# Linear attention feeding two MLPs on one core: scans read from PSUM, chunk 3 moved behind the first matmul step, VectorE priority for the first chunks, and filler matmuls in four gaps

## The chip, the core and the metric

The program runs on one NeuronCore of a Trainium2 chip. The metric is device time in microseconds (us). Six parts of the core matter here. [...] VectorE (DVE), ScalarE (ACT) and GpSimd (POOL) do elementwise work; GpSimd does not read PSUM. The queue of SyncE (SP) issues most of the DMA transfers, and each engine and queue works through its instructions in its own fixed order.

## The reference

The input has 4 batches, 8 heads, 768 positions and a head size of 48. First comes a gated linear attention, then two MLPs over the 3072 tokens (model width 384, hidden width 2048):

```python
for t in range(S):
    state = alpha[:, :, t, :, None] * state + einsum('bhd,bhe->bhde', k[:, :, t], v[:, :, t])
    y[:, :, t] = einsum('bhd,bhde->bhe', q[:, :, t], state)
x = y as (3072, 384)
h = x @ moe_w_in;   g = where(h >= 1, h, where(h <= -1, 0, (h + 1)**2 / 4));   x = g @ moe_w_out
h = x @ moe2_w_in;  g = maximum(0.01 * h, h);                                 out = g @ moe2_w_out
```

The MLP weights arrive as float64, so the kernel reads them as pairs of 32-bit words and builds float32 values itself.

## The kernel before

**Attention.** The 3072 tokens are cut into 24 chunks of 128 positions (chunk c is batch c mod 4). The recurrence becomes products of alpha inside a chunk. For a chunk, PE transposes alpha, k and q into PSUM (`transposed`, tiles `Tal`, `Tk`, `Tq`, L269). `st_alpha` copies `Tal` to the SBUF tile `al` on ACT (L278) and runs two long scans on DVE over all four head pairs at once: one backwards into `kt` (L284), one forwards into `qt` (L288), which starts from the reciprocal of the total product. The second operand of both scans is `init`, a tile of zeros whose column 0 restarts each head pair. `st_k` and `st_q` multiply `Tk` and `Tq` into `kt` and `qt`. `st_scores` multiplies `kt` and `qt` on PE (tiles `sc`) and masks them on DVE into `S` (L329). `st_ktok` transposes `kt` back, `st_kv` updates the state, and `st_y` makes the output `y` on PE (L365, L372), from which ACT and DVE build the two halves of `xt`, the input of the first MLP: first a part `xs` (L380) that six DMAs move into place (L387), then the rest (L382).

**Weights.** Each layer has 28 weight pieces in four groups: three pieces of w_in, then four of w_out in each. A piece is loaded (`raw`, four buffers), prepared by ACT (L29, L30), DVE (L31, L32) and POOL (L35), joined on DVE (L40), and split into a high and a low part by ACT and by POOL or DVE (L185, L189). One `tick` issues one stage of three neighbouring pieces.

**GEMM steps.** Three chunks make a tile of 384 tokens; a layer has eight tiles of 16 steps. Step m is nine matmuls into `h` (L445, `gemm_in`), the activation on ACT, DVE (`t`, L458), ACT and POOL into `gg`, and three steps later nine matmuls into `acc` (L485, `gemm_out`). `h` has two PSUM buffers, so the `h` of step m+2 waits until DVE has made `t` of step m. Steps 0 to 3 need the first weight group, steps 4 to 7 the second, and so on.

**What sets the order.** PE's order is written out by hand. The prelude is the string `PRE`: words such as `al.0` or `y.1` are attention stages of a chunk and `t` is a tick. Then the step loop issues gemm_out of step i-3, the planned attention stages, the hooks (ticks) and gemm_in of step i. `VISITS` puts the stages of a tile's next three chunks at half-step slots 0, 3 and 5, each chunk nine slots after the last. In the prelude `bank` hands out all eight PSUM banks in rotation; later attention has three. The order on DVE, ACT, POOL and SP is decided by a list scheduler at build time, by priority and its own estimate of times; only `st_y` raises a priority (`PRIO_Y`).

The second layer runs from about 550 us on and is not touched.

Of the kernel before, what the change touches and what calls it, by code (L numbers as in the profile page):

```python
# [7 lines left out]
F32 = mybir.dt.float32  # L8
# [4 lines left out]
ACTF = mybir.ActivationFunctionType  # L13
# [49 lines left out]
def fast_path(ctx, tc, q, k, v, alpha, w1i, w1o, w2i, w2o, out, wz, in_range):  # L63
# [55 lines left out]
    HD = H * D  # L119
    vs = [stp.tile([128, HD + X], F32, name=f"v{i}") for i in range(2)]  # L120
    nats = [stp.tile([128, 3, H, HP], F32, name=f"nat{i}") for i in range(2)]
    al = stp.tile([R, NP, C + 1], F32, name="al")
    init = stp.tile([R, NP, C + 1], F32, name="init")
    heads = [slice(HP * e, HP * e + D) for e in range(2)]

    fetched = set()
# [129 lines left out]
    def bank(nm):  # L256
# [5 lines left out]
            return ph.tile([128, 512], F32, tag="h", name=nm)  # L262
        return pa.tile([128, 512], F32, tag=f"acc{i - 5}", name=nm)

    def transposed(c, i):
        t = nats[c % 2][:, i]
        ps = bank(("Tal", "Tk", "Tq")[i])
        for a in range(NP):
            nc.tensor.transpose(  # L269
                ps[:R, a * C:(a + 1) * C],  # L270
                t[:, 2 * a:2 * a + 2, :].rearrange("p two d -> p (two d)")[:, :R],
                ident,
            )
        return ps[:R].rearrange("p (a t) -> p a t", a=NP)

    def st_alpha(c):
        ps = transposed(c, 0)
        nc.scalar.activation(out=al[:, :, 1:], in_=ps, func=ACTF.Copy)  # L278
        kt = tp.tile([R, NP, C + 1], F32, tag="kt", name="kt")
        qt = tp.tile([R, NP, C + 1], F32, tag="qt", name="qt")  # L280
        alf, inf, ktf, qtf = (t.rearrange("p a t -> p (a t)") for t in (al, init, kt, qt))
        n = NP * (C + 1)
        nc.gpsimd.memset(kt[:, NP - 1, C:], 1.0)
        nc.vector.tensor_tensor_scan(ktf[:, n - 2::-1], alf[:, n - 1:0:-1], inf[:, n - 1:0:-1], 1.0, ALU.mult, ALU.add)  # L284
        tot = tots[:, c]
        nc.vector.tensor_scalar(out=tot, in0=kt[:, :, :1], scalar1=TOT_MIN, scalar2=None, op0=ALU.max)  # L286
        nc.vector.reciprocal(out=init[:, :, :1], in_=tot)
        nc.vector.tensor_tensor_scan(qtf, alf, inf, 0.0, ALU.mult, ALU.add)  # L288
        nc.gpsimd.memset(init[:, :, :1], 1.0)
        if c >= B:  # L290
            st = states[c % B]
            for h in heads:
                nc.gpsimd.tensor_tensor(  # L293
                    out=st[h, :, h], in0=st[h, :, h], in1=tot[h].to_broadcast([D, NP, D]), op=ALU.mult
                )
        cs[c] = {"kt": kt[:, :, 1:], "qt": qt[:, :, 1:]}

    def st_k(c):
        ps = transposed(c, 1)
        kt = cs[c]["kt"]  # L300
        nc.vector.tensor_tensor(out=kt, in0=ps, in1=kt, op=ALU.mult)

    def st_q(c):
        ps = transposed(c, 2)
        load_qka(c + 2)
        qt = cs[c]["qt"]
        nc.vector.tensor_tensor(out=qt, in0=ps, in1=qt, op=ALU.mult)
# [13 lines left out]
    def st_scores(c):  # L321
        kt, qt = cs[c]["kt"], cs[c]["qt"]
        ps = [bank(f"sc{e}") for e in range(2)]
        for a in range(NP):
            for e, h in enumerate(heads):
                nc.tensor.matmul(ps[e][:, a * C:(a + 1) * C], kt[h, a, :], qt[h, a, :])  # L326
        S = sp.tile([128, 2, NP, C], F32, tag="S", name="S")
        for e in range(2):
            nc.vector.tensor_tensor(  # L329
                out=S[:, e],  # L330
                in0=ps[e].rearrange("p (a t) -> p a t", a=NP),
                in1=causal.rearrange("p (o t) -> p o t", o=1).to_broadcast([128, NP, C]),
                op=ALU.mult,
            )
# [77 lines left out]
    def stage(nm, c):  # L412
        if c < NCH:
            stages[nm](c)
# [147 lines left out]
    with tc.manual_schedule(engines={mybir.EngineType.PE}):  # L562
# [238 lines left out]
```

## Time and profile before

| | |
|---|---|
| median of three runs | 1004.99 us (1003.87 to 1006.16) |
| the profiled execution | 1004.65 us, of which the trace spans 1002.6 us |
| PE busy | 948.6 us, 95% of the span |
| DVE, ACT, POOL busy | 458.1, 476.6, 404.2 us |
| PE busy by fortieths of the span | `4567889999999999999999999999999999999997` |
| granted PE clock by fortieths | `9879889999999999999999999999999999999999` |

Each digit is a tenth of a slice of 25 us. PE is full from the seventh slice to the last; only the first six, some 130 us, have room. The share of a whole span says nothing about these six, so the rows below are by stretch.

### The profile page before, as it was taken

Reading aid. Unit: us, or ns where it says so; the run is one execution under the profiler, and the core shown is the slowest. Engines: PE = TensorE matmul, PEld = TensorE weight load, DVE = VectorE, ACT = ScalarE, POOL = GpSimd, SP = SyncE. Lnnn points to the kernel's source line nnn. Section 1 sums busy time; section 2 is a strip of 40 time slices with the busy share of each in tenths; the row PEclk is TensorE's granted clock in tenths of the full one; section 3 lists DMA queues with packets and bytes.
Section 4 is the critical chain, followed back from the end, with each engine's and each line's share of the span. In section 5 each row is a group of like instructions: output and inputs, shape, how many; then the busy total and the mean of one; then the engine's idle time right before and its main releaser. Section 6 shows DMA issues by size and latency. Waiting matters only on the chain.

```text
span 1002.6 us, 16502 instructions
## 1 busy us (share of the span) xinstructions
PE 948.6 (95%) x6226; PEld 928.2 (93%) x6226; DVE 458.1 (46%) x781; ACT 476.6 (48%) x950; POOL 404.2 (40%) x440
## 2 busy tenths in 40 slices
PE   4567889999999999999999999999999999999997
PEld 3466889999999999999999999999999999999997
DVE  6889854546555556465552455323331212121211
ACT  3566644464655555546555773333333333333332
POOL 4558853243444443435442333333333333333332
PEclk9879889999999999999999999999999999999999
DMA  9866623235443443354313435111110000000000
GB/s 171 175 160 141 151 49 64 46 97 111 110 120 84 99 124 74 106 113 118 89 39 110 130 105 172 40 56 41 56 40 32 24 1 24 1 25 1 25 1 27
DMA packets 134807, 79.02 MB, mean 79 GB/s; under 512 B 105536, under 2 KB 123456, under 8 KB 134720
## 3 DMA queue, kind: packets, MB, share of 16 engines
q1 hardware_dynamic: 122624, 52.71, 24.0%
q10 hardware_dynamic: 12096, 25.17, 8.4%
q8 instruction: 51, 0.84, 0.3%
q14 instruction: 36, 0.29, 0.1%
HBM read 59.77 MB, written 15.73 MB: 75 GB/s over the span
## 4 chain that ended last, share of the span: by engine, by line
PE 83%; DVE 7%; DMA 5%; ACT 2%; SPq 2%; issue 1%; DVEq 0%; ACTq 0%
PE h L445 37%; PE acc L487 19%; PE acc L485 18%; PE y L372 2%; PE sc L326 2%; DMA raw<-in_moe_w_in 2%; PE y L365 2%; DVE z L40 1%; DMA x2r<-x2d 1%; PE Tq L269 1%; DVE z L31 1%; DMA v<-in_v 1%; PE Tk L269 1%; PE Tal L269 1%; DVE kt L284 1%
## 5 line engine op out<-in xcount | busy, mean ns | idle before, releaser
L463 POOL TENSOR_TENSOR gg<-t,gg 128x384 fp32r<-128x384 f32 x256 | 274.7, 1074 | 458.5 <-ACT gg L462 453.5
L445 PE MATMUL h<-xt,wi 128*128 128x384 f32 x2304 | 448.5, 338 | 5.8 <-DVE t L458 3.0
L445 PEld LDWEIGHTS h<-xt,wi 128*128 128x128 f32 x2304 | 405.9, 190 | 9.2 <-DVE t L458 3.5
L485 PE MATMUL acc<-gg,wo 128*128 128x384 f32 x1152 | 227.4, 341 | 0.8 <-ACT o L498 0.8
L487 PE MATMUL acc<-wo,gg 128*128 128x384 f32 x1152 | 219.9, 334 | 0.0
L462 ACT ACTIVATE gg<-t 128x384 fp32r<-128x384 f32 x256 | 134.1, 524 | 177.3 <-DVE t L458 99.9
L485 PEld LDWEIGHTS acc<-gg,wo 128*128 128x128 f32 x1152 | 202.6, 190 | 3.4 <-ACT o L498 1.5
L487 PEld LDWEIGHTS acc<-wo,gg 128*128 128x128 f32 x1152 | 201.5, 188 | 0.0
L461 DVE TENSOR_TENSOR t<-h,t 128x384 f32<-128x384 f32 x128 | 71.1, 557 | 266.6 <-ACT t L460 266.4
L460 ACT ACTIVATE t<-h 128x384 f32<-128x384 f32 x128 | 62.9, 492 | 173.4 <-PE h L445 170.9
L458 DVE SCALAR_TENSOR_TENSOR t<-t,h 128x384 f32<-128x384 f32 x128 | 70.3, 549 | 138.4 <-ACT t L457 135.0
L456 ACT ACTIVATE t<-h,half 128x384 f32<-128x384 f32 x128 | 74.0, 578 | 94.9 <-PE h L445 93.1
L35 POOL TENSOR_TENSOR z<-z,raw 128x384 int32<-128x384 int32 (+1 forms) x56 | 67.9, 1213 | 48.6 <-DVE z L32 25.3
L457 ACT ACTIVATE t<-t 128x384 f32<-128x384 f32 x128 | 67.0, 523 | 4.0 <-ACT t L456 1.2
L284 DVE TENSOR_TENSOR_SCAN kt<-al,init 112x515 f32<-112x515 f32 x24 | 35.5, 1480 | 34.1 <-ACT al L278 34.1
L293 POOL TENSOR_TENSOR state<-state,good 48x192 f32<-48x192 f32 x40 | 26.2, 656 | 50.1 <-DVE good L286 42.9
L40 DVE SCALAR_TENSOR_TENSOR z<-raw,z 128x384 int32<-128x384 int32 (+1 forms) x56 | 41.2, 737 | 3.3 <-POOL z L35 3.3
L372 PE MATMUL y<-S,v 128*64 128x128 f32 (+1 forms) x384 | 30.4, 297 | 12.6 <-issue 5.3
L29 ACT ACTIVATE raw<-raw 128x384 int32<-128x384 uint32 (+1 forms) x56 | 33.7, 601 | 17.7 <-DMA raw<-in_moe_w_in 16.3
L31 DVE TENSOR_SCALAR z<-z 128x384 f32<-128x384 f32 (+1 forms) x56 | 27.7, 495 | 26.3 <-ACT z L30 26.2
L372 PEld LDWEIGHTS y<-S,v 128*64 128x64 f32 (+1 forms) x384 | 23.1, 139 | 17.2 <-issue 5.5
L288 DVE TENSOR_TENSOR_SCAN qt<-al,init 112x516 f32<-112x516 f32 x24 | 35.6, 1483 | 0.6
(70 smaller groups left out, 607.0 us busy)
## 6 DMA issues: line engine op xcount, KB each, us to landing
raw<-in_moe_w_out SPq DMA_DIRECT2D x16, 384.0 KB, 4.7
raw<-in_moe_w_in ACTq DMA_DIRECT2D x12, 512.0 KB, 4.3
raw<-in_moe_w_out ACTq DMA_DIRECT2D x16, 384.0 KB, 3.5
nat<-in_alpha SPq DMA_DIRECT2D x24, 192.0 KB, 3.4
nat<-in_k SPq DMA_DIRECT2D x24, 192.0 KB, 4.2
nat<-in_q SPq DMA_DIRECT2D x24, 192.0 KB, 4.4
raw<-in_moe_w_in SPq DMA_DIRECT2D x24, 192.0 KB, 4.0
v<-in_v SPq DMA_DIRECT2D x24, 192.0 KB, 3.2
```

What stands on the lines that cost most here:

```text
L35: add_eng.tensor_tensor(out=z, in0=z, in1=low, op=ALU.add)
L372: nc.tensor.matmul(y[HP * e:HP * e + n, a, :], vs[c % 2][:, (2 * a + e) * D:(2 * a + e) * D + n], d["S"][:, e, a, :], start=first and a == ...
L445: nc.tensor.matmul(h, w[:, wl, kk, f0:f0 + 128], xt[:, kk, xl, :], start=cnt == 0, stop=cnt == 3 * KD - 1,)
L456: nc.scalar.activation(out=t, in_=h, func=ACTF.Relu, bias=half, scale=0.5)
L457: nc.scalar.activation(out=t, in_=t, func=ACTF.Square)
L458: gi = nc.vector.scalar_tensor_tensor(out=g, in0=t, scalar=1.0, in1=h, op0=ALU.min, op1=ALU.max)
L460: nc.scalar.activation(out=t, in_=h, func=ACTF.Copy, scale=0.01)
L461: gi = nc.vector.tensor_tensor(out=g, in0=h, in1=t, op=ALU.max)
L462: hi = nc.scalar.activation(out=gg[:, HI], in_=g, func=ACTF.Copy)
L463: lo = nc.gpsimd.tensor_tensor(out=gg[:, LO], in0=g, in1=gg[:, HI].bitcast(F32), op=ALU.subtract)
L485: nc.tensor.matmul(acc[d][:, :N], w[:, wl, mi, d * 128:(d + 1) * 128], gg[:, xl], start=st, stop=sto)
L487: nc.tensor.matmul(acc[d][:, :DM], gg[:, xl, d * C:(d + 1) * C], w[:, wl, mi, :], start=st, stop=sto)
```

## The change

There are five edits.

1. The scans read `Tal` in PSUM. The ACT copy into `al` and the tiles `al` and `init` go. Each of the two scans becomes four scans of 128 columns, one for each head pair, with a column of zeros read with stride 0 as second operand and the start value given as an operand.
2. Chunk 3's `al k q` leave the prelude and are planned between the `h` of step 0 and step 1.
3. `BEHIND` moves the attention visits of the first three tiles back by 6, 4 and 2 half-steps.
4. In the prelude the scans, the products into `kt` and `qt` and the mask into `S` get the raised priority (`urgent`). After the prelude it has no offset.
5. Four words `w` in the prelude issue nine matmuls of the identity matrix each, into a PSUM bank that nobody reads.

```diff
+    zcol = const.tile([R, 1], F32, name="zcol")
+    zeros = zcol.to_broadcast([R, C])
...
-    al = stp.tile([R, NP, C + 1], F32, name="al")
-    init = stp.tile([R, NP, C + 1], F32, name="init")
...
+    def urgent():
+        return tc.high_priority(offset=PRIO_Y if prelude[0] else 0)
...
-        nc.scalar.activation(out=al[:, :, 1:], in_=ps, func=ACTF.Copy)
...
-        nc.vector.tensor_tensor_scan(ktf[:, n - 2::-1], alf[:, n - 1:0:-1], inf[:, n - 1:0:-1], 1.0, ALU.mult, ALU.add)
...
-        nc.vector.tensor_tensor_scan(qtf, alf, inf, 0.0, ALU.mult, ALU.add)
...
+        with urgent():
+            for a in range(NP):
+                nc.vector.tensor_tensor_scan(pad[:, a, C + 2:2:-1], ps[:, a, ::-1], zeros, 1.0, ALU.mult, ALU.add)
...
+            for a in range(NP):
+                nc.vector.tensor_tensor_scan(qt[:, a, :], ps[:, a, :], zeros, rtot[:, a, :], ALU.mult, ALU.add)
...
-        "al.0 k.0 q.0 t al.1 k.1 q.1 t kt.0 sc.0 t y.0 kv.0 al.2 k.2 q.2 t kt.1 sc.1 t y.1 kv.1 t "
-        "kt.2 sc.2 t al.3 k.3 q.3 t y.2 kv.2 t "
+        "al.0 k.0 q.0 t w al.1 k.1 q.1 t kt.0 sc.0 w t y.0 kv.0 al.2 k.2 q.2 t kt.1 sc.1 w t y.1 kv.1 t "
+        "kt.2 sc.2 t w t y.2 kv.2 t "
...
+    BEHIND = (6, 4, 2)
...
+            elif word == "w":
+                ps = bank("keep_warm")
+                for _ in range(9):
+                    nc.tensor.matmul(ps[:, :128], ident, ident)
...
-        plan = {}
+        plan = {(1, 0): [lambda w=w: stage(w, 3) for w in ("al", "k", "q")]}
...
-                    slot += i * SLOTS // n
+                    slot += i * SLOTS // n + (BEHIND[j] if j < len(BEHIND) else 0)
```

On PE before, the start of the step loop reads as follows; `wi_249` is the first group of w_in, `y<-S,v_125` belongs to chunk 3.

```order
L314 MATMUL ktok<-ident,kt 128x112 x4
L326 MATMUL sc_560<-qt,kt 128x128
L326 MATMUL sc_561<-qt,kt 128x128
...
L445 MATMUL h<-xt,wi_249 128x384 x18
L372 MATMUL y<-S,v_125 64x128
```

On PE after, the same place, right behind the last state product of chunk 2:

```order
L352 MATMUL kv<-v_125,kn 48x48
L453 MATMUL h<-xt,wi_266 128x384 x9
L272 MATMUL Tal<-ident,nat_128 112x128 x4
L272 MATMUL Tk<-ident,nat_128 112x128 x4
L272 MATMUL Tq<-ident,nat_128 112x128 x4
L453 MATMUL h<-xt,wi_266 128x384 x18
L493 MATMUL acc_738<-gg,wo_426 128x384
```

The scores of chunk 3 stood ahead of the first GEMM step; now its transposes stand behind it, and its scores behind the first `acc`.

On DVE before, these are the rows up to the last part of chunk 2's `xt`; `kt<-al` and `qt<-al` scans around them are chunk 3's, and `wi_550` and the 512-wide `z` are pieces of the second weight group.

```order
L286 TENSOR_SCALAR good<-kt 112x4
L301 TENSOR_TENSOR kt<-Tk,kt 112x4x128
L287 RECIPROCAL init<-good 112x4
L189 TENSOR_TENSOR wi_550<-z,wi_550 128x512
L288 SCALAR_TENSOR_TENSOR qt<-al,init 112x516
L31 TENSOR_SCALAR z<-z 128x512
L380 TENSOR_TENSOR xs<-y,xs 112x128
L307 TENSOR_TENSOR qt<-Tq,qt 112x4x128
L32 TENSOR_SCALAR z<-z 128x512
L382 TENSOR_TENSOR xt<-y,xt 112x3x128
```

On DVE after, the rows up to the same part of chunk 2's `xt`; `sc_482` and `sc_483` are chunk 2's scores, the first `xs` and `xt` are chunk 1's, and the 384-wide `z` are the four w_out pieces of the first group.

```order
L336 TENSOR_TENSOR S<-sc_482,causal 128x512
L387 TENSOR_TENSOR xs<-y,xs 112x128
L336 TENSOR_TENSOR S<-sc_483,causal 128x512
L40 SCALAR_TENSOR_TENSOR z<-raw,z 128x384
L389 TENSOR_TENSOR xt<-y,xt 112x3x128
L40 SCALAR_TENSOR_TENSOR z<-raw,z 128x384 x2
L189 TENSOR_TENSOR wo_426<-z,wo_426 128x384
L31 TENSOR_SCALAR z<-z 128x384
L32 TENSOR_SCALAR z<-z 128x384
L387 TENSOR_TENSOR xs<-y,xs 112x128
L40 SCALAR_TENSOR_TENSOR z<-raw,z 128x384
L389 TENSOR_TENSOR xt<-y,xt 112x3x128
```

Chunk 2's `xs` and `xt` moved ahead of chunk 3's scans and of all pieces of the second weight group.

On DVE before, at the end of the weight conversion (the last two `L40` rows; `state_121` and `xs` are chunk 5's, the first `t` is that of step 10, the `kt` scan is chunk 6's):

```order
L355 TENSOR_TENSOR state_121<-kv,state_121 48x4x48 x2
L31 TENSOR_SCALAR z<-z 128x384
L458 SCALAR_TENSOR_TENSOR t<-t,h 128x384
L380 TENSOR_TENSOR xs<-y,xs 112x128
L32 TENSOR_SCALAR z<-z 128x384
L189 TENSOR_TENSOR wo_1171<-z,wo_1171 128x384
L40 SCALAR_TENSOR_TENSOR z<-raw,z 128x384
L382 TENSOR_TENSOR xt<-y,xt 112x3x128
L40 SCALAR_TENSOR_TENSOR z<-raw,z 128x384
L284 SCALAR_TENSOR_TENSOR kt<-al,init 112x515
L458 SCALAR_TENSOR_TENSOR t<-t,h 128x384
```

On DVE after, the same end (here the `t` are those of steps 12 and 13; `state_122`, `xs` and `xt` are chunk 5's):

```order
L31 TENSOR_SCALAR z<-z 128x384
L189 TENSOR_TENSOR wo_1181<-z,wo_1181 128x384
L32 TENSOR_SCALAR z<-z 128x384
L40 SCALAR_TENSOR_TENSOR z<-raw,z 128x384
L466 SCALAR_TENSOR_TENSOR t<-t,h 128x384
L40 SCALAR_TENSOR_TENSOR z<-raw,z 128x384
L466 SCALAR_TENSOR_TENSOR t<-t,h 128x384
L362 TENSOR_TENSOR state_122<-kv,state_122 48x4x48 x2
L387 TENSOR_TENSOR xs<-y,xs 112x128
L389 TENSOR_TENSOR xt<-y,xt 112x3x128
```

At the last joined piece the order before has made `t` of steps 0 to 10, the order after those of steps 0 to 12, and chunk 5's `state`, `xs` and `xt` now stand behind it.

## Rows read from the trace of the kernel before

**Rows 1.** Busy time by stretch: start:end, length, PE, PEld, DVE, ACT, POOL, clock, DMA, GB/s
```profile
57.00:80.00 23.00, 16.73 (x99) 15.56 (x100) 21.94 (x32) 14.52 (x32) 17.55 (x15) 0.83 0.68 159
...
145.00:300.00 155.00, 155.00 (x1185) 151.01 (x1185) 81.64 (x151) 81.76 (x165) 58.53 (x73) 1.00 0.39 87
```
**Rows 2.** Waits of PE over the span: us in total, times, longest
```profile
PE Tq L269 <- DVE xt L382: 4.7, 2, 3.1
PE Tk L269 <- DVE state L355: 3.3, 1, 3.3
...
PE h L445 <- DMA xt<-xs: 2.2, 1, 2.2
```
**Rows 3.** Timeline of PE, 57 to 147 us: start, length, what, idle before
```profile
57.10 5.33 PE L445 MATMUL h<-xt,wi 128*128 128x384 f32 x18 [2.15 <-DMA xt<-xs]
...
128.60 1.10 PE L269 MATMUL Tq<-ident,nat 128*112 128x128 f32 x4 [3.07 <-DVE xt L382]
129.35 3.23 PE L485 MATMUL acc<-gg,wo 128*128 128x384 f32 x9
...
143.61 1.73 PE L485 MATMUL acc<-gg,wo 128*128 128x384 f32 x9
145.18 0.55 PE L314 MATMUL ktok<-ident,kt 112*128 112x112 f32 x4
...
146.75 1.85 PE L445 MATMUL h<-xt,wi 128*128 128x384 f32 x9
```
**Rows 4.** Timeline of DVE, 40 to 132 us
```profile
40.13 0.36 DVE L31 TENSOR_SCALAR z<-z 128x384 f32<-128x384 f32 x1 [0.56 <-ACT z L30]
40.53 0.36 DVE L32 TENSOR_SCALAR z<-z 128x384 int32<-128x384 int32 x1
...
51.58 0.28 DVE L380 TENSOR_TENSOR xs<-y,xs 112x128 fp32r<-112x128 f32 x1
...
128.47 0.88 DVE L40 SCALAR_TENSOR_TENSOR z<-raw,z 128x384 int32<-128x384 int32 x1
129.28 2.03 DVE L284 TENSOR_TENSOR_SCAN kt<-al,init 112x515 f32<-112x515 f32 x1
131.23 0.52 DVE L458 SCALAR_TENSOR_TENSOR t<-t,h 128x384 f32<-128x384 f32 x1
```
**Rows 5.** Timeline of the SP queue around 52 us
```profile
51.89 4.17 SPq L387 DMA_DIRECT2D xt<-xs  x6
```
**Rows 6.** Groups of DVE instructions by shape: busy us, mean ns, idle before
```profile
L458 DVE SCALAR_TENSOR_TENSOR t<-t,h 128x384 f32<-128x384 f32 x128 | 70.3, 549 | 138.4 <-ACT t L457 135.0 <-POOL gg L463 3.4
...
L284 DVE TENSOR_TENSOR_SCAN kt<-al,init 112x515 f32<-112x515 f32 x24 | 35.5, 1480 | 34.1 <-ACT al L278 34.1
...
L382 DVE TENSOR_TENSOR xt<-y,xt 112x384 fp32r<-112x384 f32 x24 | 13.3, 554 | 4.3 <-ACT xt L381 4.0
...
L355 DVE TENSOR_TENSOR state<-kv,state 48x192 f32<-48x192 f32 x32 | 11.2, 351 | 2.4 <-PE kv L345 2.1
...
L380 DVE TENSOR_TENSOR xs<-y,xs 112x128 fp32r<-112x128 f32 x24 | 7.0, 290 | 11.4 <-ACT xs L379 10.5 <-DMA raw<-in_moe_w_out 0.4
```
**Rows 7.** Timeline of DVE: scans of chunks 3 and 4
```profile
46.26 1.22 DVE L284 TENSOR_TENSOR_SCAN kt<-al,init 112x515 f32<-112x515 f32 x1
...
72.69 2.08 DVE L284 TENSOR_TENSOR_SCAN kt<-al,init 112x515 f32<-112x515 f32 x1
```
**Rows 8.** Timeline of a steady chunk, 157 to 166 us
```profile
157.97 0.59 ACT L278 ACTIVATE al<-Tal 112x512 f32<-112x512 f32 x1
158.10 0.60 PE L269 MATMUL Tq<-ident,nat 128*112 128x128 f32 x4
...
162.70 0.69 DVE L307 TENSOR_TENSOR qt<-Tq,qt 112x512 f32<-112x512 f32 x1
...
165.26 1.16 PE L326 MATMUL sc<-qt,kt 48*128 48x128 f32 x16
```

More of the change, by code (lines that the diff above doesn't have):

```diff
@@ L277, in st_alpha @@
         ps = transposed(c, 0)
-        nc.scalar.activation(out=al[:, :, 1:], in_=ps, func=ACTF.Copy)
[L279 to L283, printed above, removed]
-        nc.vector.tensor_tensor_scan(ktf[:, n - 2::-1], alf[:, n - 1:0:-1], inf[:, n - 1:0:-1], 1.0, ALU.mult, ALU.add)
-        tot = tots[:, c]
-        nc.vector.tensor_scalar(out=tot, in0=kt[:, :, :1], scalar1=TOT_MIN, scalar2=None, op0=ALU.max)
-        nc.vector.reciprocal(out=init[:, :, :1], in_=tot)
-        nc.vector.tensor_tensor_scan(qtf, alf, inf, 0.0, ALU.mult, ALU.add)
-        nc.gpsimd.memset(init[:, :, :1], 1.0)
+        pad = tp.tile([R, NP, C + 4], F32, tag="kt", name="kt")
+        kt = pad[:, :, 4:]
+        qt = tp.tile([R, NP, C], F32, tag="qt", name="qt")
+        nc.gpsimd.memset(kt[:, :, C - 1:C], 1.0)
+        with urgent():
+            for a in range(NP):
+                nc.vector.tensor_tensor_scan(pad[:, a, C + 2:2:-1], ps[:, a, ::-1], zeros, 1.0, ALU.mult, ALU.add)
+            tot = tots[:, c]
+            rtot = tp.tile([R, NP, 1], F32, tag="rtot", name="rtot")
+            nc.vector.tensor_scalar(out=tot, in0=pad[:, :, 3:4], scalar1=TOT_MIN, scalar2=None, op0=ALU.max)
+            nc.vector.reciprocal(out=rtot, in_=tot)
+            for a in range(NP):
+                nc.vector.tensor_tensor_scan(qt[:, a, :], ps[:, a, :], zeros, rtot[:, a, :], ALU.mult, ALU.add)
         if c >= B:
@@ L295, in st_alpha @@
                 )
-        cs[c] = {"kt": kt[:, :, 1:], "qt": qt[:, :, 1:]}
+        cs[c] = {"kt": kt, "qt": qt}
     def st_k(c):
@@ L300, in st_k @@
         kt = cs[c]["kt"]
-        nc.vector.tensor_tensor(out=kt, in0=ps, in1=kt, op=ALU.mult)
+        with urgent():
+            nc.vector.tensor_tensor(out=kt, in0=ps, in1=kt, op=ALU.mult)
     def st_q(c):
@@ L306, in st_q @@
         qt = cs[c]["qt"]
-        nc.vector.tensor_tensor(out=qt, in0=ps, in1=qt, op=ALU.mult)
+        with urgent():
+            nc.vector.tensor_tensor(out=qt, in0=ps, in1=qt, op=ALU.mult)
     def st_ktok(c):
@@ L327, in st_scores @@
         S = sp.tile([128, 2, NP, C], F32, tag="S", name="S")
[L328 to L334, printed above, removed]
+        with urgent():
+            for e in range(2):
+                nc.vector.tensor_tensor(
+                    out=S[:, e],
+                    in0=ps[e].rearrange("p (a t) -> p a t", a=NP),
+                    in1=causal.rearrange("p (o t) -> p o t", o=1).to_broadcast([128, NP, C]),
+                    op=ALU.mult,
+                )
         cs[c]["S"] = S
@@ L582, in fast_path @@
             ones.memset(t[:, 1:, :, D:], 0.0)
-        ones.memset(al[:, :, :1], 0.0)
-        ones.memset(init, 0.0)
-        ones.memset(init[:, :, :1], 1.0)
+        nc.vector.memset(zcol, 0.0)
         for t in states:
```

## The prediction, made before the changed kernel ran

> **What bounds the kernel now.** I read the busy time by stretch first. From 145 us on PE is busy for all of its 155 us at full clock, while DVE is busy 81.64 us of them [rows 1]. From there to the end the time is PE's work, which no edit changes except by stalls. Before that, in the stretch from 57 to 80 us, PE works 16.73 of 23 us and DVE 21.94 [rows 1]: DVE is what ends last there. So the change is worth what it moves in the first 146 us.
>
> The waits of PE say how DVE's load reaches it. PE stands for 4.7 us in front of `Tq` until DVE has made `xt`, for 3.3 us in front of `Tk` until DVE has added a `state`, and once for 2.2 us in front of the first `h` for the DMA of `xs` [rows 2]. These are transposes of a later chunk that want a PSUM bank which `y` or `kv` still hold, and behind them, in PE's fixed order, GEMM steps that are ready.
>
> The timeline of PE gives the marks. The first `h` starts at 57.10. The last such stall ends at 128.60, after which nine matmuls take 3.23 us where nine take 1.73 later [rows 3]. Step 16, the first of the second tile, starts at 146.75, after chunk 6's `ktok` and `sc` from 145.18 on [rows 3]. I use the start of step 16 as the yardstick, since PE is full behind it in both kernels if nothing new stalls.
>
> The timeline of DVE shows why the first `h` is late: chunk 2's `xs` runs only at 51.58, although the last piece that the new order keeps ahead of it, the fourth w_out piece of the first group, has its first DVE step at 40.13 [rows 4].
>
> **Part 1: the first GEMM step.** In the new order chunk 2's `xs` stands right behind the L31 and L32 of that piece. This piece hangs on its DMA (DVE idles before L31 for ACT, 0.56 us [rows 4]), and its load stands behind the same loads on SP as before, so I leave it at 40.13. L32 starts 0.40 later and takes 0.36: 40.9. Then `xs` 0.3, the six DMAs on SP 4.17 [rows 5], and landing: they were all issued at 51.89 + 4.17 = 56.06 and the `h` started at 57.10, so 1.04. The sum is 46.4, 10.7 us earlier than 57.10. Chunk 3's scores, which stood ahead of it on PE, are gone from there. New on SP: the first w_in piece of group two now has part of its load behind the six DMAs of chunk 2, so it comes some 4 us later and DVE idles for it; the loads behind it do not move past more than these.
>
> **Part 2: how much of this survives.** Not all of it, because DVE's work up to the end of the conversion does not shrink. `h` of step m+2 waits for DVE's `t` of step m, and DVE makes the `t` in its fixed order among the conversion. I counted DVE's rows in the order from chunk 1's first scan to the last joined weight piece: pieces, scans by chunk, masks and products are the same (the very first piece is joined just behind that scan and no longer just ahead of it), but there are two more `t`, and one `xs`, one `xt` and one pair of `state` fewer. That is 2 x 0.549 - 0.290 - 0.554 - 2 x 0.351 = -0.4 us [rows 6]. Before the first `h` both orders are held by the same DMAs. So the last piece is joined at about the same time as before, 128.47 [rows 4], and I take the same start.
>
> What differs is where PE is by then. Before, DVE had made the `t` of steps 0 to 10, and step 11's came at 131.23 [rows 4]. Now step 12's stands in front of the last piece and step 13's behind it. So step 14's `h` can start at about 128.5, and the rest runs: `h` 1.56 (nine matmuls, 143.61 to 145.18 [rows 3], also for `acc`), Tal of chunk 6 0.44, then a wait. Its `Tk` needs chunk 5's bank, so DVE's last piece (0.81 to the next start), `t` 0.5, two `state` 0.7, `xs` 0.3 and `xt` 0.56: 128.5 + 0.5 + 0.8 + 0.5 + 0.7 + 0.3 + 0.6 = 131.9. Then `Tk` and `Tq` 0.9, `acc` of step 12 1.56, `h` of step 15 1.56, `acc` of step 13 1.56, which ends at 137.5. Step 16 needs chunk 5's `xs` in place: about 131.1 + 4.17 + 1.04 = 136.3, so it is just hidden.
>
> Step 16 starts at 137.5 instead of 146.75, but chunk 6's `ktok` and `sc`, 146.75 - 145.18 = 1.57 us of PE, are still to be done. The gain is 9.25 - 1.57 = 7.7 us. `BEHIND` for the second and third tile only moves PE work between steps: nothing, as PE is full there.
>
> **Part 3: the scans.** No row shows a scan from PSUM or one of 128 columns. The lower end is a quarter of the quiet scan, 1.22 / 4 = 0.31 us each [rows 7]. The upper end is a quarter of the mean one, 1.48 / 4 = 0.37, plus all of the shortest PSUM instruction of 128 columns, `xs` with 0.29 [rows 6], as if nothing of its start overlapped: 0.66. I take 0.36, near the quarter of the mean. Four make 1.44 against 1.48: no change of DVE's sum. At 0.66 chunks 3 to 5 cost 6 x (2.64 - 1.48) = 7.0 us more and eat the gain; at 0.31 they save 1.4 us.
>
> [...]
>
> In the steady stretch the chain from `Tal` to `sc` loses the ACT copy, which starts at 157.97, and has slack: `qt` is ready at 162.70 + 0.69 = 163.39, and `sc` starts at 165.26 [rows 8], 1.9 us later. The scans may grow by 1.9 us and the 0.6 of the copy before PE waits. `Tal`'s bank is now held until the second scan; its next user, `ktok`, stands just before `sc`, which waits for a later DVE result anyway. ACT's relief of 24 x 0.6 us is worth nothing: it is not what ends last.
>
> **Part 4: priority and filler.** The priority brings forward the masks and products of chunks 0 to 2; the DMA of the fourth w_out piece decides the end of this (Part 1), so I count nothing more. The fillers are 4 x 9 matmuls in two passes each. Sixteen passes of 128 columns take 1.16 us [rows 8], so one `w` takes 1.3 us, or 2.6 at the pace of the cold nine above. Each stands where PE waits for a mask `S`, so it costs nothing, up to 1 us each if the mask is earlier, all of it ahead of a DMA that is later still. What they bring is a faster `y` in the prelude, hidden by the same DMA. The eight banks turn by one more at each `w`; the new holders that I followed are released before the instruction that PE waits for anyway.
>
> **The sum.** The profiled execution took 1004.65 us, 2.05 more than its span. 1004.65 - 7.7 = 996.95, so 997.0; its time is 0.34 below the median, which I leave out.
>
> **Rivals.**
> *A, more is kept (0.20, 992.8).* In chunk 4 the scan took 2.08 us, in chunk 3 1.22 [rows 7]: the same instruction, with POOL at work in the slow case. If reading PSUM frees the scan from that, and POOL from waiting for it, six scans gain up to 6 x (1.48 - 1.24) = 1.4 us on DVE and as much again by POOL's steps that DVE waits for; and if DVE is ahead of PE by then, the 1.4 us (130.5 to 131.9) in front of chunk 6's `Tk` go: 7.7 + 4.2 = 11.9 in all.
> [...]
> *B, less is kept (0.17, 1001.5).* The clock is low after the wait for `t` at step 14. The nine matmuls at 129.35 took 3.23 instead of 1.73 [rows 3]; two such sets cost 3.0 us, and chunk 5's `xs`, 1.2 us ahead of its need, is late by 1.5 when SP holds it behind a weight load. 7.7 - 4.5 = 3.2.
> *C, no change (0.04, 1004.5).* The first `h` is early, but DVE idles so long for chunk 3's transposes behind it and for the delayed piece that the conversion ends 6 to 8 us later. Against it: those loads were what DVE waited for before.
> *D, slower (0.09, 1011).* A scan from PSUM pays its start in full, and more: at 0.66 the gain is gone, and in the steady stretch the chain grows by 8 x 0.66 - 2 x 1.48 - 0.6 = 1.7, still within 1.9. Above 0.68 each chunk stalls PE at `sc`: at 0.72 each, by 8 x 0.72 - 2.96 - 0.6 - 1.9 = 0.3 us on the 18 chunks from chunk 6 on, 5.4 us, while the six scans in Part 3 cost 6 x (2.88 - 1.48) = 8.4 against the gain of 7.7: 1004.65 + 5.4 + 0.7 = 1010.8. For it: no row excludes such a scan. Against it: `xs` takes 0.29 from PSUM in all, its start included.
>
> **How the numbers follow.** The forecast has 0.50, from 994 to 999.5 for its own unknowns. A brings the range down to 989, B up to 1003. That leaves out most of C and D and a corner of A. A measurement of this kernel can tell about 0.2% (2 us) from no change: below 1003 is faster, which the forecast, A and nearly all of B give (0.86); C and the edge of B are the same (0.05); D is slower (0.09).
>
> **What would show it.** The first `h` near 46 us; the last joined piece near 128; step 14's `h` right behind step 12's `t`; step 16 near 137.5; scans of 128 columns near 0.36 us; no waits of PE at `sc` beyond 150 us. It is wrong if the conversion ends elsewhere than at 128, if `sc` waits in every chunk, or if step 16 waits for the DMA of `xs`.

## The result, and the profile after

The changed kernel takes 996.32 us (median of four runs, 994.5 to 996.81), the kernel before 1004.93 in the same session: a ratio of 0.9908, 95% interval 0.9891 to 0.9924. That is 8.6 us less; the forecast was 997.0. The profiled execution took 995.93 us, its span 994.2.

The busy times by stretch have the columns of [rows 1].

```profile
57.00:80.00 23.00, 16.57 (x122) 14.49 (x121) 21.27 (x34) 14.95 (x34) 19.89 (x16) 0.95 0.48 122
145.00:300.00 155.00, 155.00 (x1209) 151.00 (x1206) 83.41 (x195) 77.10 (x155) 55.48 (x68) 1.00 0.36 88
```

Behind 145 us PE (TensorE, the engine of the matrix products) is full, as it was before [rows 1], so nearly all of the 8.6 us come from ahead of it. The timeline of PE of the changed kernel shows the marks that the prediction had set.

```profile
44.98 3.22 PE L453 MATMUL h<-xt,wi 128*128 128x384 f32 x9 [8.36 <-DMA xt<-xs]
...
128.59 1.83 PE L493 MATMUL acc<-gg,wo 128*128 128x384 f32 x9
130.26 1.72 PE L453 MATMUL h<-xt,wi 128*128 128x384 f32 x9
131.82 0.60 PE L272 MATMUL Tal<-ident,nat 128*112 128x128 f32 x4
132.25 0.60 PE L272 MATMUL Tk<-ident,nat 128*112 128x128 f32 x4
...
137.81 1.72 PE L453 MATMUL h<-xt,wi 128*128 128x384 f32 x9
...
144.06 0.55 PE L320 MATMUL ktok<-ident,kt 112*128 112x112 f32 x4
```

The first `h` starts at 44.98 instead of 57.10, step 14 at 130.26, step 16 at 137.81 instead of 146.75, and chunk 6's `ktok` comes two steps behind step 16 now, no longer in front of it [rows 3]. The timeline of DVE answers to [rows 4]:

```profile
40.15 0.29 DVE L387 TENSOR_TENSOR xs<-y,xs 112x128 fp32r<-112x128 f32 x1
...
48.54 0.43 DVE L31 TENSOR_SCALAR z<-z 128x512 f32<-128x512 f32 x1 [6.11 <-ACT z L30]
...
126.45 0.55 DVE L40 SCALAR_TENSOR_TENSOR z<-raw,z 128x384 int32<-128x384 int32 x1
126.92 0.54 DVE L466 SCALAR_TENSOR_TENSOR t<-t,h 128x384 f32<-128x384 f32 x1
127.91 1.34 DVE L40 SCALAR_TENSOR_TENSOR z<-raw,z 128x384 int32<-128x384 int32 x1 [0.44 <-POOL z L35]
129.18 0.54 DVE L466 SCALAR_TENSOR_TENSOR t<-t,h 128x384 f32<-128x384 f32 x1
```

The last joined piece starts at 127.91 (128.47 before), with a `t` ahead of it and the next right behind. Every time that the forecast had set is met within 2 us. One of its signs is not met: step 14's `h` does not start right behind step 12's `t`, which is ready at 126.92 + 0.54 = 127.46, but 2.8 us later, right behind an `acc`; PE has no wait from 122.6 to 145 us. So the times alone do not show that the reasons hold, and the experiments say that some do not.

The new scans, in the groups of DVE instructions by shape:

```profile
L293 DVE TENSOR_TENSOR_SCAN qt<-Tal,rtot,zcol 112x128 f32<-112x128 f32 x96 | 38.5, 464 | 0.6
L287 DVE TENSOR_TENSOR_SCAN kt<-Tal,zcol 112x128 f32<-112x128 f32 x96 | 32.8, 405 | 24.6 <-PE Tal L272 24.1
```

These are the scans that read `Tal` in PSUM, the memory into which PE writes its products. One takes 405 or 464 ns by the mean, but four in a row overlap and take 1.36 and 1.60 us (rows further down). That is 2.96 us for a chunk, the same as two times the 1.48 of [rows 6].

A yardstick for what follows: when the `sc` of chunk 12 starts, the same PE work is behind it in every kernel here (1872 matmuls into `h`, 1890 into `acc`), whatever the order ahead of it was. This is the row of before, and then that of after.

```profile
278.85 1.16 PE L326 MATMUL sc<-qt,kt 48*128 48x128 f32 x16
```

```profile
271.49 1.16 PE L332 MATMUL sc<-qt,kt 48*128 48x128 f32 x16
```

7.4 of the profiled 8.4 us of span are made ahead of it.

### The profile page after: what moved, and what is told of

It reads as the page before. It is cut to its first block, busy times and chain, and to the rows that moved or that the text cites. A ratio compares the mean times of both kernels' runs of the same rounds, so it can differ in the third digit from the quotient of the medians.

```text
span 994.2 us, 16706 instructions
## 1 busy us (share of the span) xinstructions
PE 951.8 (96%) x6298; PEld 930.8 (94%) x6298; DVE 457.6 (46%) x926; ACT 465.6 (47%) x926; POOL 387.4 (39%) x413
## 4 chain that ended last, share of the span: by engine, by line
PE 86%; DVE 6%; DMA 5%; ACT 1%; issue 1%; SPq 0%; POOL 0%; DVEq 0%; ACTq 0%
PE h L453 38%; PE acc L495 19%; PE acc L493 19%; PE y L379 2%; PE sc L332 2%; PE y L372 2%; DVE z L40 1%; DVE z L31 1%; DMA raw<-in_moe_w_in 1%; PE Tal L272 1%; DMA x2r<-x2d 1%; PE Tq L272 1%; PE Tk L272 1%; PE kv L352 1%; DMA nat<-in_alpha 1%
## 5 line engine op out<-in xcount | busy, mean ns | idle before, releaser
L471 POOL TENSOR_TENSOR gg<-t,gg 128x384 fp32r<-128x384 f32 x256 | 268.7, 1050 | 475.7 <-ACT gg L470 455.9
L35 POOL TENSOR_TENSOR z<-z,raw 128x384 int32<-128x384 int32 (+1 forms) x56 | 67.4, 1204 | 59.3 <-DVE z L32 22.8
L287 DVE TENSOR_TENSOR_SCAN kt<-Tal,zcol 112x128 f32<-112x128 f32 x96 | 32.8, 405 | 24.6 <-PE Tal L272 24.1
L31 DVE TENSOR_SCALAR z<-z 128x384 f32<-128x384 f32 (+1 forms) x56 | 29.3, 526 | 31.7 <-ACT z L30 31.5
L40 DVE SCALAR_TENSOR_TENSOR z<-raw,z 128x384 int32<-128x384 int32 (+1 forms) x56 | 42.4, 759 | 1.4 <-POOL z L35 1.4
L297 POOL TENSOR_TENSOR state<-state,good 48x192 f32<-48x192 f32 x40 | 22.0, 551 | 45.7 <-DVE good L290 39.0
L293 DVE TENSOR_TENSOR_SCAN qt<-Tal,rtot,zcol 112x128 f32<-112x128 f32 x96 | 38.5, 464 | 0.6
L336 DVE TENSOR_TENSOR S<-sc,causal 128x512 f32<-128x512 f32 x48 | 31.0, 684 | 9.5 <-PE sc L332 9.4
L30 ACT ACTIVATE z<-raw 128x384 f32<-128x384 f32 (+1 forms) x56 | 33.2, 592 | 2.6 <-DVE wo L189 2.6
```

The costliest lines, as they stand in the source:

```text
L35: add_eng.tensor_tensor(out=z, in0=z, in1=low, op=ALU.add)
L40: nc.vector.scalar_tensor_tensor(out=z, in0=high, scalar=-0x40000000, in1=z, op0=ALU.bitwise_and, op1=ALU.bitwise_or)
L471: lo = nc.gpsimd.tensor_tensor(out=gg[:, LO], in0=g, in1=gg[:, HI].bitcast(F32), op=ALU.subtract)
```

## The experiments

Theory 1 was the prediction's: the gain is the earlier first step, kept because the `t` stand ahead of the last joined piece; scans, priority and fillers are neutral. The rival was A: the scans from PSUM stop hindering GpSimd. All twelve kernels ran beside the kernel before, in three sessions, each with its own runs of before (1005.83, 1007.03, 1005.63 us). The changed kernel was not run again in them, so what is compared with it is the ratio. The last two columns come from one profiled execution each, and that need not be a middling one: e3's is the slowest of its eleven runs (1007.11), e6's the fastest of its six (999.62). A difference of some 2 us in these columns says little.

| kernel | median us | ratio, 95% interval | first `h` | `sc` of chunk 12 |
|---|---|---|---|---|
| before (profiled) | 1004.93 | 1 | 57.10 | 278.85 |
| the change | 996.32 | 0.9908 [0.9891, 0.9924] | 44.98 | 271.49 |
| e1 no fillers | 997.07 | 0.9906 [0.9890, 0.9922] | 50.86 | 272.77 |
| e2 thin fillers | 996.39 | 0.9903 [0.9886, 0.9921] | 48.27 | 271.92 |
| e3 old scans | 1004.75 | 0.9986 [0.9977, 0.9995] | 48.63 | 281.12 |
| e4 chunk 3 in the prelude, no BEHIND | 994.00 | 0.9874 [0.9856, 0.9891] | 49.01 | 269.74 |
| e5 order edits alone | 1004.45 | 0.9976 [0.9963, 0.9989] | 53.73 | 279.25 |
| e6 new scans alone | 1000.70 | 0.9943 [0.9929, 0.9958] | 55.07 | 275.61 |
| e7 short scans from SBUF | 1013.95 | 1.0072 [1.0058, 1.0086] | 53.86 | 287.77 |
| e8 chunk 3 in the prelude | 993.30 | 0.9861 [0.9843, 0.9879] | 48.05 | 270.32 |
| e9 chunk 3 at the prelude's end | 994.36 | 0.9882 [0.9867, 0.9897] | 45.42 | 270.40 |
| e10 xs transfers on ACT's queue | 996.31 | 0.9899 [0.9886, 0.9913] | 45.38 | 272.03 |
| e11 e8 with e10's queue | 999.01 | 0.9930 [0.9917, 0.9944] | 50.11 | 274.39 |
| e12 e8 without fillers | 997.65 | 0.9918 [0.9903, 0.9933] | 55.28 | 274.44 |

Every kernel with scans from PSUM is at 0.9943 or better, every one with scans from SBUF at 0.9976 or worse.

### Are fillers worth anything? e1 and e2

e1 takes out the four words `w`; e2 keeps them with 8 columns each.

```diff
-                    nc.tensor.matmul(ps[:, :128], ident, ident)
+                    nc.tensor.matmul(ps[:, :8], ident, ident[:, :8])
```

> The changed kernel without its four groups of filler matmuls. The build-time scheduler then orders VectorE differently: chunk 2's xs stands behind 9 first steps of weight pieces and 8 joined ones (7 and 6 with the fillers), and at the last joined piece 12 t of GEMM steps are made (13 with them). Theory 1 (as predicted: what counts is where DVE's order puts chunk 2's xs and the t; the fillers' own run is worth nothing): first h near 53 us, step 16 near 141, 999 to 1000. Theory 2 (the fillers pay by keeping PE's clock up): slower by as much, but with the first h within 1 us of 45 and the matmuls of y.1, y.2 at half speed. Theory 3 (the fillers do nothing at all): 996.

> The changed kernel with fillers of 8 columns instead of 128: a sixteenth of the PE work, but the order on VectorE around chunk 2's xs and at the last joined piece keeps 7 pieces and 13 t. Theory 1: 996 (within 1.5), first h near 45. Theory 2 (the fillers' work on the chip matters): as without fillers, 999 or more, with y.1 and y.2 at half speed.

Both are at the changed kernel's time, e1 as its theory 3 had it. The fillers are not without effect on PE, though. This is chunk 1's `y` in the changed kernel, and then in e2:

```profile
29.08 0.96 PE L379 MATMUL y<-S,v 128*48 128x128 f32 x13 [0.17 <-DVE S L336]
```

```profile
31.08 2.25 PE L379 MATMUL y<-S,v 128*64 128x128 f32 x15
```

A matmul takes 74 ns behind the full fillers and 150 behind the thin ones; the granted clock of the first 42 us is 0.94 and 0.76 by the mean. That is the half speed that theory 2 named, in e1 too (15 in 2.28 us), but without its price in time. Thin fillers are hardly shorter: the second word `w` takes 2.18 us in e2 and 2.27 in the changed kernel. The first `h` is 5.9 us later in e1 and 3.3 in e2, where it was put near 45, and the time is not: the earlier first step, on which theory 1 rests, shows as 1.3 and 0.4 us at the yardstick. The order on DVE is not the same in the three, so that too is not the step alone.

### Where the gain comes from: e3, e5, e6

e3 is the changed kernel with the old scans and their copy. e5 is the kernel before with chunk 3's move and `BEHIND` only. e6 is the kernel before with the new scans only. The core of e6 (e3 is its reverse):

```diff
-        nc.scalar.activation(out=al[:, :, 1:], in_=ps, func=ACTF.Copy)
-        nc.vector.tensor_tensor_scan(ktf[:, n - 2::-1], alf[:, n - 1:0:-1], inf[:, n - 1:0:-1], 1.0, ALU.mult, ALU.add)
+            for a in range(NP):
+                nc.vector.tensor_tensor_scan(pad[:, a, C + 2:2:-1], ps[:, a, ::-1], zeros, 1.0, ALU.mult, ALU.add)
```

> The changed kernel with the old scans: ACT copies Tal to SBUF and two long scans run from there. Order on VectorE: 7 pieces ahead of chunk 2's xs, 13 t at the last joined piece, as in the changed kernel. Theory 1 (the scans are neutral, up to 1.4 us either way): 996 (994.5 to 997.5). Theory 2 (the scans from PSUM free VectorE and GpSimd from each other and carry part of the gain): 999 or more, with the last joined piece 3 us later.

> The kernel before with the order edits alone: chunk 3 behind the first GEMM step and the delayed attention visits; scans from SBUF, no priority, no fillers. VectorE has 9 pieces ahead of chunk 2's xs and 12 t at the last joined piece (before: 9 and 11). Theory 1 (as predicted, the order carries the gain): 998 to 1000. Theory 2 (after the first four runs: the scans from PSUM carry it): 1003 to 1007, with the last joined piece at 128 or later.

> The kernel before with the scans from PSUM alone: the old prelude, no delayed visits, no priority, no fillers. VectorE's order around chunk 2's xs is that of the kernel before (9 pieces; 10 t at the last joined piece). Theory 1 (the scans are neutral): 1005 (1003.5 to 1006.5). Theory 2 (the scans carry the gain in any order): 994 to 997, with the last joined piece 4 us or more ahead of the 128.5 of before.

With the old scans nearly all of the gain is gone (e3), though its first `h` is still 8.5 us earlier than before. Alone, the scans bring 0.57% (5.7 us; 6.3 by the medians), less than theory 2 had put; the order edits bring 0.24% (2.4 us, just beyond what the measurement tells apart; at the yardstick e5's profile isn't ahead of before at all). Together, in e1, 0.94%. So most of the gain comes with the scans, and theory 1 has its sum the wrong way round.

It comes with the scans, but not through their times alone. The scheduler answers to other scans with another order on DVE, ACT and POOL; PE's order stays. In e3, for instance, an L32 stands between the last two joined pieces where the changed kernel has none:

```profile
129.83 1.34 DVE L40 SCALAR_TENSOR_TENSOR z<-raw,z 128x384 int32<-128x384 int32 x1 [2.13 <-POOL z L35]
...
134.51 0.55 DVE L40 SCALAR_TENSOR_TENSOR z<-raw,z 128x384 int32<-128x384 int32 x1
134.98 0.35 DVE L32 TENSOR_SCALAR z<-z 128x384 int32<-128x384 int32 x1
...
136.53 1.33 DVE L40 SCALAR_TENSOR_TENSOR z<-raw,z 128x384 int32<-128x384 int32 x1
```

The last piece comes at 136.53, 8.6 us later than in the changed kernel and 8.1 later than before. These are the waits in e3 between 42 and 137 us (total, times, longest), and behind them the one line that answers to them in the changed kernel:

```profile
PE sc L332 <- DVE qt L313: 12.3, 3, 5.7
...
DVE z L40 <- POOL z L35: 4.3, 2, 2.1
```

```profile
PE sc L332 <- DVE qt L313: 4.1, 1, 4.1
```

The wait of DVE for POOL's L35 is 0.4 us in the changed kernel. Adding the groups of DVE up to the last piece, e3 and the changed kernel differ by 1.7 us in busy time (119.6 and 117.9 us) and by 5.5 us in idle time (27.5 and 22.0).

The closest pair is e5 and e1, which differ by the scans: the orders on PE and SP are the same, and up to the last piece DVE makes 28 pieces, six chunks' scans and 12 `t` in both. The last piece comes at 127.31 in e5 and at 122.43 in e1. DVE is busy for 119.1 and 118.6 us and idle for 18.9 and 15.4. It saves 4.1 us on scans and `good` and spends nearly as much more on other instructions. POOL does its 58 larger instructions (L35, L189 and `gg`) in 77.4 and in 72.6 us. Its splits, in e5 and then in e1:

```profile
L189 POOL TENSOR_TENSOR wi<-z,wi 128x512 fp32r<-128x512 f32 x8 | 12.8, 1605 | 1.5 <-ACT wi L185 1.5
L189 POOL TENSOR_TENSOR wo<-z,wo 128x384 fp32r<-128x384 f32 x10 | 12.4, 1237 | 6.0 <-ACT wo L185 5.9
```

```profile
L189 POOL TENSOR_TENSOR wi<-z,wi 128x512 fp32r<-128x512 f32 x8 | 11.2, 1399 | 1.9 <-ACT wi L185 1.9
L189 POOL TENSOR_TENSOR wo<-z,wo 128x384 fp32r<-128x384 f32 x10 | 10.6, 1064 | 6.2 <-DMA xt<-xs 3.1 <-ACT wo L185 3.0
```

So it is not DVE's own work that shrinks, but POOL's, and what DVE stands and waits for. No run holds the order on all engines, or keeps ACT's copy while the scans read PSUM, so how much of the gain is freed instructions, how much another order and how much the missing copy isn't shown.

### Short scans or PSUM? e7

e7 keeps the changed kernel's eight short scans but lets them read a copy of `Tal` in SBUF.

```diff
...
+        nc.scalar.activation(out=al, in_=ps, func=ACTF.Copy)
...
-                nc.vector.tensor_tensor_scan(pad[:, a, C + 2:2:-1], ps[:, a, ::-1], zeros, 1.0, ALU.mult, ALU.add)
+                nc.vector.tensor_tensor_scan(pad[:, a, C + 2:2:-1], al[:, a, ::-1], zeros, 1.0, ALU.mult, ALU.add)
...
```

> The changed kernel with its eight short scans, but reading an SBUF copy of Tal that ACT makes: split and column of zeros kept, only the source moved back. VectorE's order: 9 pieces ahead of chunk 2's xs, 12 t at the last joined piece. Theory A (two SBUF inputs hold VectorE and GpSimd against each other; the source in PSUM is what pays): scans of 128 columns stretch from 0.4 us to 0.6 or more where GpSimd works, 1002 to 1006. Theory B (the split into short scans or the column of zeros pays): 996 to 998, scans at 0.40 and 0.46 throughout.

It is slower than before, and slower than theory A had put. The order on DVE, ACT and POOL is again another one, but the scans' own rows need no comparison of orders. At their quickest four in a row are as long as from PSUM (1.37 and 1.61 us, in the changed kernel 1.36 and 1.60), but at their longest they take 4.01 and 4.03. In the changed kernel none of the scans takes more than 426 or 485 ns. Up to the last joined piece the 48 scans take 30.6 us in e7, against 9.6 + 8.2 = 17.8 in the changed kernel:

```profile
L295 DVE TENSOR_TENSOR_SCAN qt<-al,rtot,zcol 112x128 f32<-112x128 f32 x24 | 16.0, 725 | 0.1
L289 DVE TENSOR_TENSOR_SCAN kt<-al,zcol 112x128 f32<-112x128 f32 x24 | 14.6, 668 | 4.4 <-ACT al L282 4.4
```

One row of the timeline, with POOL beside it:

```profile
60.83 1.26 POOL L35 TENSOR_TENSOR z<-z,raw 128x384 int32<-128x384 int32 x1 [1.18 <-DVE z L32]
61.12 4.01 DVE L289 TENSOR_TENSOR_SCAN kt<-al,zcol 112x128 f32<-112x128 f32 x4
62.04 1.15 POOL L473 TENSOR_TENSOR gg<-t,gg 128x384 fp32r<-128x384 f32 x1
63.15 1.39 POOL L190 TENSOR_TENSOR wi<-z,wi 128x512 fp32r<-128x512 f32 x1
```

Four scans take 4.01 us instead of 1.36: 2.65 more, while POOL runs three instructions. The changed kernel has the same neighbourhood, with nothing lost on either side:

```profile
49.34 1.36 DVE L287 TENSOR_TENSOR_SCAN kt<-Tal,zcol 112x128 f32<-112x128 f32 x4
49.64 1.29 POOL L35 TENSOR_TENSOR z<-z,raw 128x512 int32<-128x512 int32 x1 [6.06 <-DVE z L32]
```

In the kernel before, the times of such neighbours add up as if the two took turns:

```profile
13.93 1.61 POOL L35 TENSOR_TENSOR z<-z,raw 128x512 int32<-128x512 int32 x1 [1.19 <-DVE z L32]
14.32 2.32 DVE L284 TENSOR_TENSOR_SCAN kt<-al,init 112x515 f32<-112x515 f32 x1
...
15.51 2.85 POOL L189 TENSOR_TENSOR wi<-z,wi 128x512 fp32r<-128x512 f32 x1
...
16.56 0.66 DVE L40 SCALAR_TENSOR_TENSOR z<-raw,z 128x512 int32<-128x512 int32 x1
17.14 1.25 DVE L286 TENSOR_SCALAR good<-kt 112x4 f32<-112x4 f32 x1
```

The scan is issued at 14.32; POOL's L35 runs until 13.93 + 1.61 = 15.54. If the scan starts only then and takes its quiet 1.22 [rows 7], it ends at 16.76; the row says 16.64. POOL's next, L189, is issued at 15.51 and takes 1.66 in the changed kernel at this place, beside the same L40 of DVE (1.28 is its shortest in the kernel before); from 16.64 on that ends at 18.30, the row says 18.36. And `good`, 4 columns that take 0.16 us elsewhere, ends at 18.39, with it. By this sum, an estimate from these rows, the scan waits out L35, L189 the scan, and `good` L189, each a whole instruction; so the times add up, and both engines lose. The L40 at 16.56 takes 0.66 us, so the rows do not show it of every instruction. What in an instruction decides it was not shown either. The length of the short scans goes with their source: beside L35 four take 1.36 us from PSUM and 4.01 from SBUF. That two SBUF inputs are the cause, as theory A has it, is not shown: `good` reads one tile, `kt` in SBUF, and still took 1.25 us. The scans are not the only instructions with such a spread: L40, which reads the SBUF tiles `raw` and `z`, still takes from 0.54 to 1.78 us in the changed kernel, and its last two, of one shape, 0.55 and 1.34 (126.45 and 127.91 above).

### What chunk 3's move and BEHIND are worth: e4, e8, e9

e8 puts chunk 3's `al k q` back into the prelude; e4 also sets `BEHIND` to zero; e9 puts them at the prelude's very end.

```diff
-        "kt.2 sc.2 t w t y.2 kv.2 t "
+        "kt.2 sc.2 t al.3 k.3 q.3 w t y.2 kv.2 t "
...
-        plan = {(1, 0): [lambda w=w: stage(w, 3) for w in ("al", "k", "q")]}
+        plan = {}
```

> The changed kernel with chunk 3 back in the prelude and no delay of the attention visits (scans from PSUM, priority and fillers kept). VectorE then makes 8 scans into kt and 6 xt by the last joined piece instead of 6 and 5, so that piece ends 6 to 9 us later. Theory 1: about half of the gain is lost, 1000 (998 to 1003), with stalls of PE in front of Tk and Tq as before. Theory 2 (scans, priority and fillers carry the gain): 996 to 997.

> The changed kernel with chunk 3 back in the prelude but the delayed visits kept. The old order with everything else changed took 994.0, the changed kernel 996.3. If moving chunk 3 is what costs these 2 us: 994. If the delay of the visits costs them: 996.3. VectorE's order has 7 pieces and 13 t, as in the changed kernel.

> Chunk 3's three stages go back into the prelude, but to its very end, behind chunk 2's y and ahead of the first GEMM step; all else as in the changed kernel. The question is what moving chunk 3 costs (the kernel with chunk 3 at its old place in the prelude took 0.986 of before, the changed kernel 0.991). Theory 1 (what counts is that chunk 3's scans and products fill VectorE's idle time ahead of the first step, which is 6.1 us long at 42 to 48 in the changed kernel, instead of coming between the pieces behind it): ratio 0.986, about 993 us, and step 16 no later than 137.8. Rival (what counts is chunk 3's place ahead of chunk 2's y, where TensorE's 40 us of prelude have room for its transposes): no gain, ratio 0.991, about 997 us, with the first step later by the transposes' time.

e8 is faster than the changed kernel (its interval lies below; 3 us in the medians, 1.2 at the yardstick). e4 and e9 have lower ratios too, but their intervals touch the changed kernel's. e4 came out below both of its theories: without two of the five edits the kernel is at least as fast. e4 and e8 differ by less than can be told, so `BEHIND` is worth nothing that shows with chunk 3 in the prelude. e9 hints at why moving chunk 3 costs. DVE of e9 ahead of the second weight group:

```profile
40.25 0.26 DVE L387 TENSOR_TENSOR xs<-y,xs 112x128 fp32r<-112x128 f32 x1
40.43 1.59 DVE L293 TENSOR_TENSOR_SCAN qt<-Tal,rtot,zcol 112x128 f32<-112x128 f32 x4
...
42.86 0.68 DVE L313 TENSOR_TENSOR qt<-Tq,qt 112x512 f32<-112x512 f32 x1
43.98 0.43 DVE L31 TENSOR_SCALAR z<-z 128x512 f32<-128x512 f32 x1 [0.45 <-ACT z L30]
```

Chunk 3's scans and products run where DVE of the changed kernel was about to idle for 6.11 us, the first `h` is as early as there (45.42 against 44.98), step 16 starts at 136.72, and the pieces behind have DVE to themselves. The wait for the weight piece went too: its last load comes ahead of the six transfers of `xs` here, behind them there. e9 changes both at once, so how much each of them is worth stays open; the next experiment was meant for the second. e8 has the lowest ratio of all, 0.9861.

### Is it the transfers on SyncE's queue? e10 and e11

In the changed kernel SP issues the six transfers ahead of the last load that the piece needs:

```profile
40.46 4.23 SPq L394 DMA_DIRECT2D xt<-xs  x6
44.74 0.58 SPq L165 DMA_DIRECT2D raw<-in_moe_w_in  x1
```

e10 gives these six to ACT's queue, e11 does so in e8.

```diff
-                    nc.sync.dma_start(
+                    (nc.scalar if c == 2 else nc.sync).dma_start(
```

> The changed kernel with the six small transfers of chunk 2's xt issued by ScalarE instead of SyncE. In the changed kernel they stand on SyncE's queue (40.46 to 44.69) ahead of the last load of the next group's first weight piece, and VectorE waits 6.1 us for that piece. Theory 1 (that late piece is what moving chunk 3 costs): VectorE's wait falls to 2 us or less, the last joined piece comes 3 to 4 us earlier (124), ratio 0.986 to 0.988. Rival (the piece is hidden behind the first steps, or ScalarE's own work is delayed by as much by issuing them): ratio 0.991 or above, 996 us or more.

> The changed kernel with chunk 3 back at its old place in the prelude, and with the six transfers of chunk 2's xt on ScalarE's queue. Theory 1 (two independent costs, late weight piece and chunk 3's place): faster than either alone, ratio 0.982 to 0.985, about 990 us. Rival (with chunk 3 in the prelude VectorE's wait for the piece is filled already): ratio 0.986, 993 us, as without the other queue.

Neither kernel gains what its theory 1 had put, but e10 does not test its own: the wait that should have gone stayed. In e10 ACT's queue issues them until 39.53 + 6.11 = 45.64, and ACT is the engine that prepares the piece next (timeline of e10):

```profile
39.53 6.11 ACTq L394 DMA_DIRECT2D xt<-xs  x6
46.08 0.68 ACT L29 ACTIVATE raw<-raw 128x512 int32<-128x512 uint32 x1 [6.07 <-DMA raw<-in_moe_w_in]
```

The row names the load as what ended ACT's wait, yet it starts right behind the last issue, so either may have been last. DVE still idles 5.88 us, to 47.36. Whether the piece would be earlier with the transfers out of both ways wasn't tried. e11 is slower than e8, by 4.1 us at the yardstick and 5.7 in the medians. Its order of DVE differs from e8's as well (one `t` fewer ahead of the last piece), so that the queue alone is to blame isn't shown.

### Fillers once more: e12

e12 is e8 without the words `w`.

> The changed kernel with chunk 3 back at its old place in the prelude and without the unread matmuls; VectorE then joins 8 pieces instead of 7 ahead of chunk 2's xs. Theory 1 (the unread matmuls matter only through the order that they lead to, and in the order with chunk 3 in the prelude that is worth several us, as the two kernels at 0.987 and 0.994 that differ by them alone suggest): ratio 0.991 to 0.994, 997 to 1000 us. Rival (worth nothing, as in the changed kernel itself): ratio 0.986, 993 us.

As theory 1 said: 0.9918 against 0.9861, 4.1 us at the yardstick. The build-time scheduler counts the fillers as PE work and puts DVE's instructions in another order: 9 pieces have their L31 ahead of chunk 2's `xs` instead of 7, and the first `h` waits until 55.28 instead of 48.05. The pair e6 and e4 has the same distance, 0.9943 and 0.9874, but differs by the priority as well, which in e4 does change the order on DVE, ACT, POOL and SP; the two were not tried apart. In the changed kernel the same shift costs nothing that shows (e1).

## Why the prediction was right, and where it was wrong

**Part 1 holds.** The first `h` was put at 46.4 and came at 44.98. Half of the difference is `xs`, which ran at 40.15 instead of 40.9, since the L31 ahead of it came at 38.86 and not at 40.13; the other half is the landing, 0.3 us behind the last issue (40.46 + 4.23 = 44.69) and not 1.04. The idle time for the late weight piece came too, with 6.11 us.

**Part 2 was right by its number and failed in its reason.** "So the last piece is joined at about the same time as before" came true (127.91 against 128.47). It rested on DVE's work being equal in the two orders, and that is so: 119.8 us of busy time up to the last piece before, 117.9 after. But equal work does not fix the end. With 118.6 to 119.6 us of it the last piece comes at 122.43 in e1, 127.31 in e5 and 136.53 in e3, with 15.4, 18.9 and 27.5 us of idle time. What the idle time behind the first steps becomes was not worked out; that before and after have 21.4 and 22.0 us of it is luck. The forecast also put the whole gain down to the order and the scans at nothing, and e3, e5 and e6 show the reverse. The end of the path was wrong too. Step 14 did not wait for DVE's `t` but for PE's own work ahead of it, 1.8 us later than put, and the wait that was worked out in front of chunk 6's `Tk` did not come (132.25 in the rows above, no idle time). These two misses offset each other, and step 16 came within 0.3 us.

**Part 3 was right by DVE's own time and missed the rest.** The eight scans take 2.96 us per chunk, forecast 2.88, before 2.96. Four were put at 1.44, and take 1.36 (the first scans) and 1.60 (the second): one takes more by the mean, 0.40 and 0.46, than the 0.36 of the forecast, but four in a row overlap. What "no change of DVE's sum" left out is all that comes with other scans besides their own time; in e6 that is 5.7 us.

**Part 4.** In the changed kernel the priority does nothing: with an offset of zero the order on all five engines stays as it is. The fillers' run time is worth nothing and they bring a faster `y` that is hidden, both as put; one `w` takes 2.27 us, the first 3.48, where 1.3 to 2.6 was given. Their effect on the scheduler, 4.1 us between e12 and e8, was not seen.

**The rivals.** A had 0.20, and what it assumed is seen in the rows: beside L35 four scans take 1.36 us from PSUM, and POOL's L189 at 15.5 takes 1.66 where it took 2.85. Its price was put on top of 7.7; in truth the scans bring most of the 8.6, with what the scheduler makes of them. A sized it by the scans (1.4 us) and as much again by POOL. By the groups between 42 and 137 us, before and after, the scans and `good` of four chunks take 16.0 and 12.5 us. Beside them the picture is mixed: POOL's split of a w_out piece falls from 1514 to 1195 ns by the mean, its split of a w_in piece rises from 1430 to 1543, and DVE's L40 of 512 columns from 907 to 1129. B's low clock isn't there (the `acc` behind `Tq` takes 1.81 us, and the granted clock from 130 to 137 us is 1.00), nor is a wait for `xs` at step 16. D is out: no scan is over 0.49 us, and behind 145 us PE of the changed kernel has no wait at `sc`; the only one listed is this.

```profile
PE h L453 <- DVE t L469: 1.1, 1, 1.1
```

The chain there, in the changed kernel's steady chunk, has more room than before [rows 8]:

```profile
161.07 0.69 DVE L313 TENSOR_TENSOR qt<-Tq,qt 112x512 f32<-112x512 f32 x1
...
164.15 1.16 PE L332 MATMUL sc<-qt,kt 48*128 48x128 f32 x16
```

`qt` is done at 161.76, 2.4 us ahead of `sc`, where it was 1.9.

## What to carry to other kernels

Where VectorE and GpSimd work side by side, look at the longest and shortest of one shape before counting means: the first scan goes from 1.22 to 2.32 us in the kernel before, and four short ones from 1.37 to 4.01 in e7, where in the rows shown GpSimd was at work in the long cases. With `Tal` read from PSUM the spread of a scan was 0.39 to 0.43 and 0.45 to 0.49 us. Equal work on the bounding engine does not fix its end; its idle time has to be followed too, and a forecast that hits should still be taken apart, since errors can cancel. When a scheduler sets the order, any edit, even work that nobody reads, can act through it: compare orders before explaining times, and between experiments as well.

## What the runs showed of the hardware

What a scan and a GpSimd instruction lose beside each other was not expected in this size. In the rows at 13.93 to 18.39 it is, by the estimate above, the other's whole length; four scans of 128 columns go from 1.37 to 4.01 us in e7, and a 4-column instruction from 0.16 to 1.25 in the kernel before. No instruction of GpSimd in the traces of before and after has a PSUM tile among its operands. A scan that takes its start value from a tile is 0.06 us longer than one with a constant (449 against 392 ns at the shortest, in the changed kernel), though here the direction of the scan differs too. Six transfers took ACT's queue 6.11 us to issue where SP's took 4.23, and 3.8 to 4.9 for the other sets of six in the changed kernel up to 160 us. Matmuls of 8 columns, each with its own weight load, were hardly faster than those of 128: 2.18 and 2.27 us for the second `w`, though 2.17 and 3.48 for the first.
